# A second condition on when VectorE score tiles are held back, with a share of 0.29 and eight played orders

## The chip, the cores and the metric

The kernel runs on one core of a Trainium2 chip. The core has TensorE (PE, matrix products into PSUM banks), ScalarE (ACT), VectorE (DVE), GpSimd (POOL), and SyncE (SP), which here only issues DMAs. Each engine takes its own instructions in the order in which they were written, and waits on semaphores for the others. The metric is the device time of one execution in microseconds; it is the median of several runs.

## The reference

The inputs are 2048 rows of 640 numbers for each of two independent parts, and the output sets the two results side by side.

Part A is a state-space layer (SSM). With 640 complex states, it computes for every row t

```
h_t = Lam_bar * h_(t-1) + B_bar x_t          (one complex recurrence for each state)
y_t = 2 Re(C h_t) + Dskip * x_t
```

Part B is attention with 32 query heads of 20 numbers and a single key and value head for all of them:

```
scores = q k^T / sqrt(20)      32 heads x 2048 queries x 2048 keys
p = softmax(scores);  o = p v;  result = o wo
```

The exponential over 32 x 2048 x 2048 scores is most of the elementwise work; everything that multiplies goes through TensorE.

## The kernel before

**Tiles.** The scores are cut into 2048 tiles of 128 keys x 512 queries. There are 32 blocks (four spans of 512 queries by eight groups of four heads), and a block has 16 key chunks x 4 heads = 64 tiles. `tile_n` counts the tiles that have been handed out so far. TensorE computes up to three score tiles at once, side by side in its rows, into a PSUM tensor of three banks called SC; this is a *fill*, and there are two such tensors that take turns. A profile shows a fill as three SC matmuls.

**Two ways to the exponential.** Most tiles are done by ScalarE: one ACTIVATE (L1213) reads two or three banks of SC, takes the exponential, and writes bf16 to PR. The other tiles are done by VectorE, by an approximation in integers: a TENSOR_SCALAR (L652, by way of `fill_d`, L1390) turns a score into the bits of a bf16 number, a power of two with a straight line between. Three more copies of this tile with other integers added (`copy`, L1493) are made by POOL (INT64_ADD, L1507, two tiles at a time) or by VectorE, and a weighted sum over the four is close to the exponential. The weights are folded into four scaled copies of the values (VS). These tiles lie in BIG, in slots called DR: 20 at first and 41 later (`NDS`, `MORE`); one VectorE tile takes four of them until its products are done.

**Products.** TensorE multiplies each exponentiated tile by the values (PV): one matmul for a ScalarE tile (PR with VP), four for a VectorE tile (BIG with VS). Each such matmul uses 32 of the array's columns, and four of them, one for each head of the block, run side by side into one bank.

**The SSM part** is cut into 4 spans of 512 rows by 5 groups of 128 states. One such *unit* (`unit_task` L2009, `unit_rest` L2032) is a series of matmuls (xaT with BA and BT), and then on VectorE: the product with a table (prod<-MB,tab), an addition, two scans (L2041), the carry (ctmp, hst), a second product with the table, an edge column (L2067, or a MEMSET L2070 in the first span), and last the addition into W. Output products with C (`y_task`, L2090) follow. Units, output products, projections and softmax sums are *tasks*; most of them share one PSUM bank (MB), one after another (`manager`, L2224). Before the first unit, C is scaled on VectorE in some forty steps (`scale_c`, L1948).

**The order of the work is played out before the kernel is written.** `Schedule` (L49 on) is a planner: it has a duration for every step, and for each engine it picks, at each moment, the step with the lowest priority number whose operands are there. A fill has 0, a VectorE tile in a fill's third bank (`P1OWN`) 0.42, a task's matmuls 0.95, PV products 2.0 (0.9 when buffers run short). What the planner finds is the fixed order of each engine's instructions on the chip. `planned` (L493) plays the order from several seeds; each seed but the first moves the due times of tasks by up to 12 tiles at random. It keeps the one whose end is earliest by the planner's own durations.

**When VectorE gets a tile.** For every fill, `want_own` (L1262) decides whether the third bank goes to VectorE (then ScalarE takes two banks) or to ScalarE (then it takes three). It says no when the VectorE tiles so far would pass `SHARE` x (tile_n - 16), when two earlier ones still wait, when four slots aren't free, and when `behind` (L1273) is true. `want_d` (L1351), for a VectorE tile in the one free MB bank, has the same conditions on share, slots and `behind`. Each unit has a due time in tiles: 260 for the first, and then some 43 or 87 tiles apart up to 1693. `behind` is true when `tile_n` is more than `LAG` = 120 past the due time of the first unit whose last step (the addition into W) hasn't started. While it is true, no VectorE tile is begun. `hurry` (L2081) marks the SSM steps of a unit as `late` from 40 tiles past its due time; the steps that scale C are marked from tile 150. A late step moves ahead of most other VectorE work.

`Schedule.ready(op)` (L117) gives the time from which a step's operands are there, or None as long as some step that it needs hasn't been begun. It doesn't ask for a step's gate (a condition such as a free buffer).

Of the kernel before, what the change touches and what calls it, by code (L numbers as in the profile page):

```python
# [406 lines left out]
S, D, NC, H, DH = 2048, 640, 5, 32, 20  # L407
# [8 lines left out]
class Build:  # L416
# [4 lines left out]
    NRD = 3  # L421
    NDS = 20
    MORE = 21
    SHARE = 0.28

    SHIFTS = ((0, 0.2421875), (32, 0.201171875), (64, 0.169921875), (96, 0.142578125))

# [60 lines left out]
        self.early = [b for b in self.banks if b not in rest]  # L488

    SPREAD = 12.0  # L490
    PLANS = 4

    def planned(self):  # L493

        best = None
        for seed in range(self.PLANS):
            plan = copy.copy(self)
# [764 lines left out]
    def want_own(self):  # L1262
        if self.tile_n >= NTILE - self.LAST or self.d_count + 1 > self.SHARE * (self.tile_n - 16) or self.behind():
            return False
        if sum(1 for o in self.firsts if o.start is None) >= self.WAITING:
            return False
        self.firsts = [o for o in self.firsts if o.start is None]
        return len(self.d_free()) > len(self.SHIFTS) - 1
# [4 lines left out]
    def behind(self):  # L1273

        while self.next_unit < NQB * NC:
            w = self.w_op.get(divmod(self.next_unit, NC))
            if w is None or w.start is None:
                return self.tile_n > self.unit_due[divmod(self.next_unit, NC)] + self.LAG
            self.next_unit += 1
        return False  # L1280

# [69 lines left out]
    def want_d(self, taken=0, own=0):  # L1351
        s = self.s
        if self.tile_n >= NTILE - self.LAST or self.d_count + taken + own + 1 > self.SHARE * (self.tile_n - 16):
            return False
# [944 lines left out]
```

## Time and profile before

| | |
|---|---|
| median of three runs | 734.45 us (734.43 to 736.88) |
| the profiled execution | 734.64 us; its span 732.8 us |
| PE matmul, busy | 708.3 us (97%) |
| PE weight load, busy | 253.0 us (35%) |
| ACT, busy | 712.4 us (97%) |
| DVE, busy | 602.0 us (82%) |
| POOL, busy | 408.8 us (56%) |
| ACTIVATE PR<-SC over two banks, over three banks | 509 and 169 instructions (and one over a single bank) |
| VectorE tiles (TENSOR_SCALAR BIG<-SC and BIG<-MB) | 485 + 37 = 522 of 2048 |

The profiled execution took 0.19 us more than the median, and 1.8 us of it lie outside the span. Two engines are busy almost throughout, so that neither total tells which of them sets the pace. The ends of matmuls in a trace are modelled, and instructions of ACT and DVE overlap a little with the next (a duration includes the way in and out); starts are the safer thing to measure. A window's table gives for each engine its busy time and in brackets the number of instructions.

### The profile page before, as it was taken

How to read it: one execution, taken by the hardware profiler on the slowest of the kernel's cores; microseconds unless marked ns; L12 is line 12 of the kernel's file. 1: busy time of each engine (PE TensorE's matmuls, PEld its weight loads, DVE VectorE, ACT ScalarE, POOL GpSimd, SP SyncE). 2: the span in 40 equal slices, each digit the busy share in tenths (PEclk: the TensorE clock that was granted, in tenths of full speed). 3: DMA queues.
4: the chain of work that ended last, by engine and by line, in shares of the span. 5: the costliest groups of instructions: out<-in, count | busy, mean ns of one | idle time of the engine just before them, and what ended most of it. 6: DMA issues, size and time to landing. Idle time of an engine off the chain costs nothing.

```text
span 732.8 us, 26675 instructions
## 1 busy us (share of the span) xinstructions
PE 708.3 (97%) x11268; PEld 253.0 (35%) x11271; DVE 602.0 (82%) x1178; ACT 712.4 (97%) x703; POOL 408.8 (56%) x686
## 2 busy tenths in 40 slices
PE   8999999998999999999999999999999999999997
PEld 4322223233443432333333333233333333342233
DVE  7767999897677697778988998988889998876873
ACT  6899999999999999999999999999999999999995
POOL 3366564530046377586663746566645665687860
PEclk9799999999999999999999999999999999999999
DMA  9403543366121010100110010101100001100001
GB/s 204 68 27 107 133 110 99 76 138 97 31 60 26 13 30 24 38 23 18 40 41 23 16 26 26 42 21 34 34 20 10 19 8 40 37 24 18 19 21 38
DMA packets 78090, 34.44 MB, mean 47 GB/s; under 512 B 58852, under 2 KB 77972, under 8 KB 77972
## 3 DMA queue, kind: packets, MB, share of 16 engines
q1 hardware_dynamic: 76352, 32.34, 18.6%
q8 instruction: 90, 1.47, 0.8%
q10 hardware_dynamic: 1620, 0.39, 0.3%
q14 instruction: 28, 0.23, 0.1%
HBM read 11.53 MB, written 9.75 MB: 29 GB/s over the span
## 4 chain that ended last, share of the span: by engine, by line
ACT 52%; PE 45%; DVE 2%; DMA 1%; issue 1%; ACTq 0%
ACT PR L1213 51%; PE MB L637 16%; PE SC L637 15%; PE MB L633 12%; PE SC L633 1%; DMA BIG<-in_B_wq_dram 1%; DVE prod L647 0%; DVE BIG L652 0%; DVE mab L887 0%; DVE pvsb L647 0%; PE SC L929 0%; ACTq L618 0%; DVE g L2041 0%; DVE QT L652 0%; DVE pvsb L1574 0%
## 5 line engine op out<-in xcount | busy, mean ns | idle before, releaser
L1213 ACT ACTIVATE PR<-SC 128x1024 bf16<-128x1024 f32 (+1 forms) x679 | 697.5, 1239 | 5.1 <-PE SC L637 3.6
L1507 POOL INT64_ADD BIG<-BIG x659 | 397.9, 619 | 292.5 <-DVE BIG L652 171.8
L652 DVE TENSOR_SCALAR BIG<-SC 128x512 int16<-128x512 f32 x485 | 325.8, 686 | 70.1 <-PE SC L637 64.3
L637 PE MATMUL SC<-QT,KT 32*128 32x512 bf16 x2011 | 267.1, 386 | 14.6 <-ACT PR L1213 10.1
L637 PE MATMUL MB<-BIG,VS 128*32 128x512 bf16 x2088 | 244.0, 384 | 0.0
L637 PE MATMUL MB<-PR,VP 128*32 128x512 bf16 x1526 | 211.6, 386 | 0.5 <-DVE pvsb L1574 0.3
L637 PEld LDWEIGHTS SC<-QT,KT 32*128 32x128 bf16 x2011 | 68.0, 91 | 254.4 <-ACT PR L1213 178.1
L637 PEld LDWEIGHTS MB<-BIG,VS 128*32 128x32 bf16 x2088 | 59.1, 95 | 64.8 <-issue 47.3
L637 PEld LDWEIGHTS MB<-PR,VP 128*32 128x32 bf16 x1526 | 51.6, 95 | 54.8 <-issue 41.5
L652 DVE TENSOR_SCALAR BIG<-BIG 128x1024 int16<-128x1024 int16 (+1 forms) x136 | 48.8, 405 | 7.6 <-PE MB L637 5.7
L633 PE MATMUL MB<-CT,W 128*32 128x320 bf16 (+2 forms) x1040 | 51.4, 301 | 0.8 <-DVE prod L647 0.5
L633 PE MATMUL MB<-xaT,BT 128*32 128x256 bf16 x800 | 35.4, 275 | 0.0
L647 DVE TENSOR_TENSOR prod<-MB,tab 128x1024 bf16<-128x1024 f32 x20 | 24.3, 1217 | 13.0 <-PE MB L633 12.9
L633 PE MATMUL MB<-xaT,BA 128*32 128x256 bf16 x800 | 32.7, 274 | 0.0
L633 PE MATMUL MB<-CA,W 128*32 128x512 bf16 (+1 forms) x640 | 32.0, 302 | 0.7 <-issue 0.4
L652 DVE TENSOR_SCALAR BIG<-MB 128x512 int16<-128x512 f32 x37 | 25.2, 682 | 3.7 <-PE MB L637 2.4
L633 PE MATMUL MB<-WO,OP 128*32 128x128 bf16 (+1 forms) x576 | 27.8, 297 | 0.2 <-DVE pvsb L647 0.2
L633 PEld LDWEIGHTS MB<-CT,W 128*32 128x32 bf16 x1040 | 20.9, 96 | 18.2 <-issue 10.2
L633 PE MATMUL MB<-BIG 128*32 128x512 bf16 x340 | 26.7, 397 | 0.0
L1755 DVE CAST stg<-MB 128x512 bf16<-128x512 f32 x35 | 23.9, 683 | 1.7 <-PE MB L633 1.3
L1574 DVE CAST pvsb<-MB 128x512 bf16<-128x512 f32 x31 | 21.2, 684 | 3.8 <-PE MB L637 3.7
L2041 DVE TENSOR_TENSOR_SCAN g<-sc,hst,prod 128x256 bf16<-128x256 f32 x30 | 22.3, 754 | 0.1
(162 smaller groups left out, 388.2 us busy)
## 6 DMA issues: line engine op xcount, KB each, us to landing
out_dram<-stg SPq DMA_DIRECT2D x31, 128.0 KB, 1.8
qd<-BIG SPq DMA_DIRECT2D x20, 128.0 KB, 1.9
QT<-qd SPq DMA_DIRECT2D x28, 80.0 KB
OP<-pvsb SPq DMA_DIRECT2D x105, 20.0 KB
rdP<-recs SPq DMA_DIRECT2D x105, 20.0 KB
W<-in_A_B_re_dram SPq DMA_DIRECT2D x10, 160.0 KB, 2.6
W<-in_A_B_im_dram SPq DMA_DIRECT2D x10, 160.0 KB, 2.6
lbd<-W SPq DMA_DIRECT2D x10, 160.0 KB, 2.4
```

The source lines that it names most:

```text
L633: r = e.matmul(out[32 * j:32 * j + 32], lhsT=lhsT[:, 32 * j:32 * j + 32], rhs=rhs, start=start, stop=stop, tile_position=(0, 32 * j), skip ...
L637: return lambda e: e.matmul(out, lhsT=lhsT, rhs=rhs, start=start, stop=stop, **kw)
L647: return lambda e: e.tensor_tensor(out, a, b, op)
L652: return lambda e: e.tensor_scalar(out, a, s1, s2, op0=op0, op1=op1)
L1213: ex = self.act(lambda e: e.activation(dst, t[:, 0:512 * n], ACT.Exp, scale=1.0 / UNIT), 0.8333 * 512 * n + 64, table="exp", deps=[op], re ...
L1507: op.fns.append(lambda e: e.int64_add(words(dst), words(src), add))
L1574: ev = self.dve(lambda e: e.tensor_copy(p.pvsb[:, slot, :], bank.ap), 645, deps=[op], reads=[bank.key], writes=[f"pvsb{slot}", f"pvsb{slot ...
L1755: ev = self.dve(lambda e: e.tensor_copy(st, bank.ap), 645, deps=[prev], reads=[bank.key], writes=[key], prio=self.EV, gate=(lambda: last.e ...
L2041: o = self.dve(lambda e, ri=ri, init=init: e.tensor_tensor_scan(p.g[:, u, ri, :], rdec, p.prod[:, 1, 0, ri, :], init, ALU.mult, ALU.add), ...
```

## The change

The two limits on the planner are new (share 0.29 for 0.28, eight seeds for four), and `behind` has a second condition: besides the unit being more than 120 tiles past due, some step that waits in VectorE's list must be marked late and have all its operands begun. Where the late unit's steps aren't there yet (their matmuls haven't run, so that the first product isn't begun), VectorE tiles are no longer held back. No instruction is new. What changes is how many tiles VectorE does, when, and with it the whole planned order.

```diff
-    SHARE = 0.28
+    SHARE = 0.29
...
-    PLANS = 4
+    PLANS = 8
...
         while self.next_unit < NQB * NC:
             w = self.w_op.get(divmod(self.next_unit, NC))
             if w is None or w.start is None:
-                return self.tile_n > self.unit_due[divmod(self.next_unit, NC)] + self.LAG
+                return self.tile_n > self.unit_due[divmod(self.next_unit, NC)] + self.LAG \
+                    and any(o.late and self.s.ready(o) is not None for o in self.s.pending["dve"])
             self.next_unit += 1
         return False
```

## The prediction

> **What bounds the kernel now.** I read first the engines' totals, then the forms of ScalarE's instruction, then a table of windows, and last the order of VectorE and of PE inside them.
>
> ```profile
> L1213 ACT ACTIVATE PR<-SC 128x1024 bf16<-128x1024 f32 x509 | 480.5, 1119 | 4.9 <-PE SC L637 3.6 <-PE MB L637 0.3
> L1213 ACT ACTIVATE PR<-SC 128x1536 bf16<-128x1536 f32 x169 | 236.9, 1606 | 0.2 <-PE MB L637 0.2
> ```
>
> These are ScalarE's exponentials by shape. In the order of time one starts a median of 0.904 us after a two-bank one (mean 0.935) and 1.33 us after a three-bank one: 509 x 0.935 + 169 x 1.335 = 701.5 us, and they run from 20.4 to 721 us. ScalarE is thus never free, and a fill with a VectorE tile in it (two banks for ScalarE) is 1.335 - 0.935 = 0.40 us shorter than one without.
>
> ```profile
> core 0: us, PE busy (x) PEld busy (x) DVE busy (x) ACT busy (x) POOL busy (x), PEclk, DMA share, GB/s
> 80.00:120.00 40.00, 37.29 (x485) 11.51 (x481) 37.29 (x76) 39.96 (x39) 21.49 (x35) 1.00 0.45 118
> 120.00:153.50 33.50, 32.80 (x431) 9.62 (x428) 29.01 (x56) 32.92 (x33) 21.12 (x35) 1.00 0.41 93
> 153.50:178.00 24.50, 19.50 (x313) 7.84 (x305) 22.73 (x49) 24.50 (x20) 0.00 (x0) 1.00 0.63 122
> 178.00:204.00 26.00, 24.62 (x519) 12.37 (x516) 15.25 (x35) 26.00 (x21) 0.00 (x0) 1.00 0.23 52
> 204.00:720.00 516.00, 510.03 (x8426) 182.03 (x8422) 433.23 (x786) 514.39 (x512) 325.23 (x539) 1.00 0.10 26
> ```
>
> In these windows ACT and PE are both full; from 204 us on PE idles 6.0 us in 516. Is PE's busy time real? Its order at 686 us:
>
> ```profile
> 686.14 0.39 PE L637 MATMUL SC<-QT,KT 32*128 32x512 bf16 x3
> 686.46 0.61 PE L637 MATMUL MB<-BIG,VS 128*32 128x512 bf16 x8
> 687.01 0.39 PE L637 MATMUL SC<-QT,KT 32*128 32x512 bf16 x3
> 687.33 0.83 PE L633 MATMUL MB<-CA,W 128*32 128x512 bf16 x12
> 688.10 0.39 PE L637 MATMUL SC<-QT,KT 32*128 32x512 bf16 x3
> ```
>
> Fills are 0.87 and 1.09 us apart: 0.32 for the scores, 0.55 for eight matmuls (two rounds of four) and 0.77 for twelve. A round of four is 0.77 - 0.55 = 0.22 us, and changing between scores and the rest costs about 0.11 each way. Nothing is left between them. The hold looks like this on VectorE:
>
> ```profile
> 151.51 0.68 DVE L652 TENSOR_SCALAR BIG<-SC 128x512 int16<-128x512 f32 x1
> ...
> 177.55 0.49 DVE L647 TENSOR_TENSOR CT<-W,CT 128x640 bf16<-128x640 bf16 x1
> 178.00 0.06 DVE L2070 MEMSET W<- 128x2 bf16 x1
> 181.44 1.23 DVE L647 TENSOR_TENSOR prod<-MB,tab 128x1024 bf16<-128x1024 f32 x1 [3.37 <-PE MB L633]
> ...
> 185.81 0.42 DVE L647 TENSOR_TENSOR W<-prod 128x512 bf16<-128x512 bf16 x1
> 186.18 0.06 DVE L2070 MEMSET W<- 128x2 bf16 x1
> 186.65 0.69 DVE L1574 CAST pvsb<-MB 128x512 bf16<-128x512 f32 x1 [0.41 <-PE MB L637]
> 189.71 1.23 DVE L647 TENSOR_TENSOR prod<-MB,tab 128x1024 bf16<-128x1024 f32 x1 [2.37 <-PE MB L633]
> ...
> 203.85 0.68 DVE L652 TENSOR_SCALAR BIG<-SC 128x512 int16<-128x512 f32 x1
> ```
>
> No VectorE tile for 52 us. Counting tiles by their starts, tile 380 (due time 260 + 120) falls at 153.5 us, and every later hold too begins where the count passes a unit's due time + 120: 210, 225, 240.5, 271, 301, 330, 386, 444, 527 and 587 us.
>
> **Part 1, the condition.** A held stretch opens only where no late step has its operands begun. From 153.5 to 178 us the scaling of C is a chain in which the next step is always ready: no change there. After that a unit's column step is ready at once but takes 0.06 to 0.16 us; what opens is the wait for the unit's matmuls: 178.1-181.4, 186.2-189.7, 194.3-197.6, then 240.5-248.4 (product at 248.36) and 527-532 us. In the other holds the first product starts before or within 3 us of the hold's start, so a late step is ready throughout. At one fill per 0.94 to 1.33 us that is 3 + 3 + 3 + 7 + 3 = 19 more fills with a VectorE tile.
> - On ScalarE: 19 x 0.40 = 7.6 us less. This is the one end.
> - On PE: each such tile has four products in place of one, three quarters of a round: 0.75 x 0.22 = 0.16 us, together 3.0 us more. This is the other end, if PE alone sets the pace.
> - Each tile takes 0.40 + 0.16 = 0.56 us of PE's time, and PE idles 1.4 us in 178-204, 0.03 in 240.5-253 and nothing in 527-538. That feeds 2.5 tiles: 2.5 x 0.40 = 1.0 us. The other tiles are paid back: their products queue behind tasks, slots come free later, and later fills are refused. I take **-1.0 us**, nearest to PE's row, because it has no idle time to give.
> - On VectorE each tile is 0.69 us (19 x 0.69 = 13 us), in stretches where it idles 3.4 + 2.8 + 3.1 us and more. Queued behind such a tile are the unit's first product and the PV bank's copy to pvsb: at worst 0.69 us late in five gaps, 3.4 us of delay to the SSM chain. That lengthens holds by as much, about three tiles or 1.2 us in ScalarE's terms, nothing in PE's.
> - POOL gets 19 x 3 / 2 x 0.62 = 18 us of copies, hidden (it stood still for these 52 us). SP gets no new DMA and none is moved in its queue by this condition itself; the issues of sums and OP wait for pvsb alone, by the same 0.69 us at most.
>
> A rule is to be weighed here. The Trainium skill (Perfetto Trace Analysis, Identifying the Most-Contended Engine) says that TensorE's headroom is not to be judged by its matmul busy share but by that of the weight loads. That is 253.0 of 732.8 us, 35%, which leaves room, and by the rule part 1 would be worth its whole 7.6 us. The rows at 686 us differ: starts follow each other with nothing between, so I go by them.
>
> The same skill (SBUF — State Buffer, Who interferes with whom) speaks against the change: VectorE with two SBUF inputs and a GpSimd op that reads SBUF exclude each other for a whole instruction. The trace has one: OP<-OP,rdP took 0.66 us at 241.06, while POOL's INT64_ADD of 0.61 began at 240.83, against a mean of 0.43. By the rule alone a unit's second step would be blocked up to 0.62 us in each of the five gaps, 3.1 us in the SSM chain; by the row 0.23 x 5 = 1.2 us.
>
> **Part 2, the share.** At 40, 80, 120 and 160 us the count of VectorE tiles is 6, 37, 70 and 96 at tiles 42, 160, 283 and 393, below 0.28 x (tile - 16) by 1, 3, 5 and 10; from 200 us on by 35 to 53. Up to three tiles are handed out and not begun, so the limit binds until about 130 us and never after. 0.29 allows 0.01 x (393 - 16) = 3.8 tiles more: bounds 0 and -1.5 us (3.8 x 0.40), or +0.6 us by PE's 0.16. PE idles 2.7 + 0.7 us in 80-153.5, enough for six. But only 20 slots are there then. I take two tiles, **-0.8 us**.
>
> **Part 3, the orders.** No row shows another order. What an order can change is how far ScalarE's starts are stretched over 0.904 and 1.33: 0.4 to 1.6 us in a stretch of 40 us, a spread of about 0.4, so 0.4 x sqrt(18) = 1.7 us for a whole order. Bounds: -1.7 and +1.7 us (the planner chooses by its own durations, and the new condition reshuffles every seed). The best of eight instead of four: I take **-0.5 us**, a third of it.
>
> **Sum**: -1.0 - 0.8 - 0.5 = -2.3 us. The profiled execution goes from 734.64 to 732.3; it stood 0.19 above the median, so the median goes from 734.45 to **732.1 us**, with a range of its own of 729.5 to 735 (order +-1.7, share 0 to -1.5).
>
> **The rivals.**
> - *ScalarE is the bound after all.* For it: ACT's 514.39 of 516 us, and PE takes its tasks only in the holes left by fills. Each tile also brings the due times 0.40 us nearer, and the holds at 210, 225, 271, 301 us, which don't open, grow; I take off 6 tiles: 13 x 0.40 + 1.5 + 0.5 = 7.2 us, **727.2 us**.
> - *PE's debt (slower).* For it: PE's 510.03 of 516 us, and the last SSM output product still runs at 708 us, so work put off has nowhere to go. If slots don't refuse the later tiles and VectorE goes toward its new limit, 0.29 x 2012 = 583 tiles, there are up to 61 more: 61 x 0.16 = 9.8 us. I take half, 30 tiles: +4.8, **739.3 us**. It decides once tiles begun beyond the 2.5 that idle time feeds exceed about 15 (15 x 0.16 = 2.4 us, which eats the sum above). Against it: slots have kept the count 50 under the old limit.
> - *The condition does next to nothing.* `ready` ignores gates, and an edge column or a waiting step of the next unit may keep it true in the planner's time. Then parts 2 and 3 remain: 733.1; without an effect of the share, **734 us**.
>
> **How the numbers follow.** Likeliest 0.38; ScalarE bound 0.25; PE's debt 0.22; nothing 0.15. About 0.5% (3.7 us) is what a measurement here can tell from no change: faster means under 730.8, slower over 738.1. Faster: 0.23 of the 0.25 and 0.10 of the 0.38, 0.33. Slower: 0.18 of the 0.22 and 0.03 from an order that falls badly, 0.21. The rest, 0.46, is the same. The range takes in most of ScalarE's case and half of PE's: 726.5 to 739.5 leaves out about 0.08 below and 0.11 above.
>
> **What the next profile would show.** Step 1 right: VectorE tiles between 178 and 204 us, about nine, and between the column step and the first product of later units; still none from 153 to 178. The payback: the total stays near 522 to 530, PE's idle time in 178-204 is gone, ACT two-bank starts are stretched more than 0.935. ScalarE's case: over 535 tiles, and still 0.935. PE's debt: the last SSM output product later than 709 us against the end of the exponentials, or a longer tail than 12 us. The share: a count of VectorE tiles two to four higher at tile 283. The prediction is wrong if PE has room that its starts hide, or if the new order shifts something outside these terms, in the first 40 us or in the tail.

## The result, and the profile after

The changed kernel takes 732.06 us (median of 18 runs, 730.51 to 734.83). The kernel before, run again on the same chips beside it, takes 735.52 us (18 runs, 733.18 to 739.5). The ratio is 0.9953, with a 95% interval of 0.9936 to 0.9969: 3.5 us less, within the 0.5% that the prediction called no difference, though the interval leaves 1 out. At equal granted clock of TensorE it is 4.2 us less (how this is reckoned stands at the head of the experiments). The profiled execution took 732.94 us, its span 731.2 us.

Which steps moved? First the forms of ScalarE's exponential in the kernel after (count | busy us, mean ns | idle before, releasers):

```profile
L1213 ACT ACTIVATE PR<-SC 128x1024 bf16<-128x1024 f32 x517 | 489.7, 1120 | 5.2 <-PE SC L637 4.6 <-PE MB L637 0.2
L1213 ACT ACTIVATE PR<-SC 128x1536 bf16<-128x1536 f32 x162 | 228.4, 1584 | 0.0
```

Eight more fills are of two banks and seven fewer of three (509 and 169 before). The starts are as far apart as they were: a mean of 0.9354 us after a two-bank one and 1.3324 after a three-bank one. 516 x 0.9354 + 162 x 1.3324 = 698.5 us (the last of the 517 has no next start), against 701.3 before (509 x 0.9346 + 169 x 1.3350; the prediction's 701.5 comes from rounded means). ScalarE's own list is thus 2.8 us shorter. The two profiled spans differ by 1.6 us only (732.8 and 731.2), since in the profile after the list begins 1.5 us later, at 21.9 us for 20.4: from 10 to 20 us its granted clock is 0.85, where it was 1.00 before. VectorE does 492 + 36 = 528 tiles, six more than before.

The table of windows, after, with the same windows as in the prediction:

```profile
core 0: us, PE busy (x) PEld busy (x) DVE busy (x) ACT busy (x) POOL busy (x), PEclk, DMA share, GB/s
80.00:120.00 40.00, 34.66 (x455) 10.73 (x447) 39.19 (x81) 40.00 (x40) 20.30 (x34) 1.00 0.47 108
120.00:153.50 33.50, 32.18 (x410) 10.21 (x411) 32.48 (x63) 33.28 (x33) 18.95 (x32) 1.00 0.40 101
153.50:178.00 24.50, 22.03 (x306) 7.42 (x299) 22.89 (x56) 24.50 (x20) 0.00 (x0) 1.00 0.67 128
178.00:204.00 26.00, 25.17 (x507) 12.28 (x505) 21.26 (x42) 26.00 (x23) 5.97 (x10) 1.00 0.28 64
204.00:720.00 516.00, 512.66 (x8485) 182.03 (x8486) 429.96 (x765) 515.07 (x512) 335.76 (x556) 1.00 0.10 26
```

From 204 us on PE idles 3.3 us in 516, where it idled 6.0 before; ACT is as full as it was. In 178 to 204 us there are 23 ACTIVATEs where there were 21, and POOL, which stood still there, makes ten copies: VectorE tiles begin in the old hold. They show in VectorE's order, after:

```profile
181.66 0.49 DVE L647 TENSOR_TENSOR CT<-W,CT 128x640 bf16<-128x640 bf16 x1
182.88 0.69 DVE L652 TENSOR_SCALAR BIG<-SC 128x512 int16<-128x512 f32 x1 [0.73 <-PE SC L637]
184.22 0.69 DVE L652 TENSOR_SCALAR BIG<-SC 128x512 int16<-128x512 f32 x1 [0.65 <-PE SC L637]
185.31 0.69 DVE L652 TENSOR_SCALAR BIG<-SC 128x512 int16<-128x512 f32 x1 [0.39 <-PE SC L637]
185.91 1.22 DVE L647 TENSOR_TENSOR prod<-MB,tab 128x1024 bf16<-128x1024 f32 x1
187.05 0.68 DVE L652 TENSOR_SCALAR BIG<-SC 128x512 int16<-128x512 f32 x1
...
192.00 0.42 DVE L647 TENSOR_TENSOR W<-prod 128x512 bf16<-128x512 bf16 x1
```

The hold opens as soon as C is scaled (CT<-W,CT ends at 182.15) and the first unit's product isn't there yet. Three tiles go in front of this product and a fourth behind it. The same chain ran from 177.55 (CT<-W,CT) by 181.44 (product) to 185.81 (W<-prod) before: now the first unit is done at 192.0, 6.2 us later. Of these, 2.5 us have nothing to do with the tiles: the kernel with the share alone (e2) has C scaled 2.5 us earlier than this one, and this one is behind it by the same 2.5 us at tile 50 already.

### The profile page after: what moved, and what is told of

It reads as the page before. It is cut to its first block, busy times and chain, and to the rows that moved or that the text cites. A ratio compares the mean times of both kernels' runs of the same rounds, so it can differ in the third digit from the quotient of the medians.

```text
span 731.2 us, 26574 instructions
## 1 busy us (share of the span) xinstructions
PE 709.3 (97%) x11222; PEld 252.0 (34%) x11225; DVE 606.2 (83%) x1175; ACT 709.7 (97%) x703; POOL 418.3 (57%) x701
## 4 chain that ended last, share of the span: by engine, by line
ACT 55%; PE 41%; DVE 1%; DMA 1%; issue 0%; ACTq 0%; POOL 0%
ACT PR L1213 55%; PE MB L637 14%; PE SC L637 14%; PE MB L633 12%; DMA BIG<-in_B_wq_dram 1%; PE SC L633 1%; DVE BIG L652 0%; PE SC L929 0%; DVE mab L887 0%; POOL BIG L1508 0%; ACTq L618 0%; DVE QT L652 0%; DVE brow L652 0%; DVE pvsb L1575 0%; DVE BA L1720 0%
## 5 line engine op out<-in xcount | busy, mean ns | idle before, releaser
L1508 POOL INT64_ADD BIG<-BIG x674 | 407.5, 620 | 280.4 <-DVE BIG L652 143.9
L652 DVE TENSOR_SCALAR BIG<-SC 128x512 int16<-128x512 f32 x492 | 330.6, 686 | 83.6 <-PE SC L637 78.5
L637 PE MATMUL MB<-BIG,VS 128*32 128x512 bf16 x2112 | 255.9, 384 | 0.2
L637 PE MATMUL MB<-PR,VP 128*32 128x512 bf16 x1520 | 217.9, 388 | 0.2 <-ACT PR L1213 0.2
L637 PEld LDWEIGHTS MB<-BIG,VS 128*32 128x32 bf16 x2112 | 62.9, 95 | 68.6 <-issue 46.4
L652 DVE TENSOR_SCALAR BIG<-BIG 128x1024 int16<-128x1024 int16 (+1 forms) x127 | 46.3, 408 | 4.1 <-PE MB L637 3.4
L633 PE MATMUL MB<-xaT,BA 128*32 128x256 bf16 x800 | 35.3, 274 | 0.0
L633 PE MATMUL MB<-WO,OP 128*32 128x512 bf16 (+1 forms) x512 | 25.6, 306 | 0.0
L633 PEld LDWEIGHTS MB<-xaT,BA 128*32 128x32 bf16 x800 | 19.6, 96 | 9.6 <-issue 6.3
```

What stands on the lines that cost most here:

```text
L633: r = e.matmul(out[32 * j:32 * j + 32], lhsT=lhsT[:, 32 * j:32 * j + 32], rhs=rhs, start=start, stop=stop, tile_position=(0, 32 * j), skip ...
L637: return lambda e: e.matmul(out, lhsT=lhsT, rhs=rhs, start=start, stop=stop, **kw)
L652: return lambda e: e.tensor_scalar(out, a, s1, s2, op0=op0, op1=op1)
L1508: op.fns.append(lambda e: e.int64_add(words(dst), words(src), add))
```

## The experiments

All the comparisons are with the kernel before, run in the same set: medians of 735.62 us (26 runs) for the first four kernels, 736.25 (10) for the next four and 735.82 (18) for the last four. The planner's own end is given too. It isn't a measured time but the moment at which the last step ends by the planner's durations, 723.12 us for the kernel before.

The theory at the start was the prediction's: PE is the bound, a VectorE tile is paid only out of PE's idle time, and the condition is worth little because the rest is paid back. The rivals were that ScalarE is the bound and more VectorE tiles are worth their 0.40 us; and that the gain is not of the condition at all, but of another order or of the share.

**The granted clock.** One thing differs between executions of the same kernel and has to be taken off before small differences are read. In every profile TensorE's granted clock (PEclk) stands at 0.50 for a stretch that begins between 25 and 29 us, and its length varies. The window from 24 to 44 us of the kernel before, of e1, of e2 and of the kernel after, in turn:

```profile
core 0: us, PE busy (x), PEclk, DMA share, GB/s
24.00:44.00 20.00, 19.62 (x207) 0.74 0.18 47
24.00:44.00 20.00, 19.62 (x223) 0.83 0.19 49
24.00:44.00 20.00, 19.62 (x211) 0.74 0.18 41
24.00:44.00 20.00, 19.38 (x188) 0.66 0.15 30
```

That is about 10.4, 6.8, 10.4 and 13.6 us at half clock ((1 - 0.74) x 2 x 20 = 10.4). The time follows: of the 54 executions of the kernel before that have their clock on record, the one with the lowest mean clock (0.985) took 739.85 us, the eleven with the highest (0.995) a median of 733.97. One straight line fitted to all 157 executions, with a level for each kernel, gives 0.51 us for each 0.001 of mean clock and leaves a scatter of 0.55 us. On it the three chips agree within 0.4 us for the kernel before. The executions of two kernels don't have the same clock on average (0.9888 in e2, 0.9926 in the kernel before beside it). So the differences are also given at equal clock, by this line, uncertain by 0.3 to 0.5 us at 95% (0.8 in e5 and e6, which have two executions, and 0.7 in e8; the profiles of e5 and e8 have a second stretch at half clock near 180 us, whose price isn't shown). Why the stretch is longer in one execution than in another, and whether a kernel's own order has a part in it, isn't shown.

### The condition alone (e1_condition, e9_condition_order2)

```diff
 # the kernel after
-    SHARE = 0.29
+    SHARE = 0.28
-    PLANS = 8
+    PLANS = 4
```

> The second condition alone: share 0.28 and four seeds, as before. Theory PE (TensorE sets the pace, tiles let through are paid back later): some seven more VectorE tiles in 178-204 us and ten in 240-253, most of them missing again within 40 us, total 524 to 530; 1 to 2.5 us faster than before. Rival ScalarE (each tile kept is worth 0.40 us and nothing has to be paid back): over 535 tiles and 5 us or more. Rival that the gain came from the choice among orders and the share: no faster than before, +-1 us.

Measured: 732.8 us, ratio 0.996 (0.9946 to 0.9974), 2.9 us less (2.5 at equal clock). The planner kept its order 3, with 528 tiles. The kernel before has order 2, so the same comparison was made at this order:

```diff
 # the kernel after
-    SHARE = 0.29
+    SHARE = 0.28
-        for seed in range(self.PLANS):
+        for seed in (2,):
```

> The condition alone, share 0.28, with the order of seed 2, the seed that the kernel before keeps, so that the tasks' due times are jittered alike. Theory: the condition is worth 1 to 3 us in any order; the planner's own end is 1.0 us earlier than that of the kernel before: 0.5 to 2 us faster. Rival: what the condition alone gained came from another order: +-0.5 us.

Measured: 734.07 us, ratio 0.9972 (0.9955 to 0.9988), 2.1 us less (1.5 at equal clock), with 523 tiles.

The condition by itself is worth 2 to 3 us; at equal clock 1.5 to 2.5 of the 4.2. Where does it come from? VectorE's instructions that read SC, in the windows around the openings; e1 first:

```profile
core 0: us, DVE busy (x), PEclk, DMA share, GB/s
178.00:204.00 26.00, 5.57 (x9) 1.00 0.19 44
204.00:240.50 36.50, 14.52 (x22) 1.00 0.15 37
240.50:253.00 12.50, 6.02 (x9) 1.00 0.04 10
253.00:280.00 27.00, 10.69 (x16) 1.00 0.09 19
527.00:538.00 11.00, 3.84 (x6) 1.00 0.07 15
```

and the kernel after:

```profile
178.00:204.00 26.00, 5.51 (x8) 1.00 0.28 64
204.00:240.50 36.50, 12.33 (x18) 1.00 0.15 37
240.50:253.00 12.50, 7.57 (x12) 1.00 0.05 11
253.00:280.00 27.00, 10.06 (x15) 1.00 0.09 19
527.00:538.00 11.00, 4.98 (x9) 1.00 0.04 10
```

The kernel before has 1, 27, 1, 22 and 1 in these windows. The three openings that the prediction named are there, with 8 + 8 + 5 = 21 more tiles in e1 and 7 + 11 + 8 = 26 after. The window behind each of the first two has fewer: 22 and 16 for 27 and 22 in e1, 18 and 15 after. At the end six tiles are left.

The time at which a given tile starts tells the same. All numbers are differences to the kernel before in us (the fill that holds the tile), and in brackets the difference in VectorE tiles begun by then:

| tile | e1, condition | after |
|---|---|---|
| 50 | -1.2 (0) | +2.7 (+1) |
| 300 | -1.2 (0) | -0.3 (+7) |
| 500 | -4.0 (+7) | -2.0 (+8) |
| 700 | -5.2 (+9) | -1.8 (+8) |
| 1000 | -2.0 (+3) | +1.7 (+1) |
| 1400 | -0.1 (-1) | +2.0 (0) |
| 1500 | -3.5 (+5) | -1.0 (+6) |
| 2040 | -3.9 (+6) | -1.4 (+6) |

(At tile 50, where no VectorE tile is held yet, e1's profiled execution was 1.2 us ahead and the one after 2.7 behind, in step with the half-clock stretches above. From there to tile 2040 e1 gains 2.7 us and the kernel after 4.1.) The openings at 178 to 248 us bring 4 us by tile 700 in e1, and by tile 1400 they are given back whole. The opening at 527 us takes 3.0 to 3.4 us off the stretch from tile 1400 to 1500 (35.4 us before, 32.0 in e1, 32.4 after), and nothing takes this back: from tile 1500 to 2040 it is 175.9 us in both, 176.3 before. So in these two kernels the net gain is that of the last opening. It isn't so in every order. In e9 the three windows hold 9, 12 and 7 tiles and the stretch from tile 1400 to 1500 is 3.5 us shorter too, but 3.1 of them are gone again at tile 2040; in e3 (the kernel after in another order, below) the stretch is 0.9 us shorter and 0.8 are gone. What decides whether this gain stays isn't shown. In e1 and after, the units behind it are not late: the additions into W at 536.5 and 559.7 us before are at 536.6 and 557.7 in e1, at 532.2 and 550.6 after, and so no hold that follows gets longer.

What pays back? Not the slots. In the planner, the answers to the question whether VectorE may have the third bank were:

```
                yes   no: held   no: two waiting or no slots
before          475         89                            69
after           480         92                            60
condition (e1)  487         96                            52
```

(Five and four are refused for the share, before and after.) The openings take some 20 refusals off the hold's 89, and yet it ends with more; the slots refuse fewer. The units are later, so the following holds are longer: the first eight additions into W are at 185.8, 193.9, 202.0, 215.3, 230.2, 252.2, 275.0 and 304.6 us before; at 188.3, 195.5, 205.3, 218.9, 228.1, 254.6, 278.4 and 310.5 in e1; at 192.0, 198.8, 207.3, 222.7, 234.1, 257.0, 279.1 and 312.6 after. Why they are later shows in VectorE's order in e1:

```profile
176.32 0.49 DVE L647 TENSOR_TENSOR CT<-W,CT 128x640 bf16<-128x640 bf16 x1
177.37 0.69 DVE L652 TENSOR_SCALAR BIG<-SC 128x512 int16<-128x512 f32 x1
178.90 0.69 DVE L652 TENSOR_SCALAR BIG<-SC 128x512 int16<-128x512 f32 x1 [0.84 <-PE SC L637]
179.77 0.69 DVE L652 TENSOR_SCALAR BIG<-SC 128x512 int16<-128x512 f32 x1 [0.18 <-PE SC L637]
180.76 0.69 DVE L652 TENSOR_SCALAR BIG<-SC 128x512 int16<-128x512 f32 x1 [0.29 <-PE SC L637]
181.37 1.21 DVE L647 TENSOR_TENSOR prod<-MB,tab 128x1024 bf16<-128x1024 f32 x1
182.50 0.68 DVE L652 TENSOR_SCALAR BIG<-SC 128x512 int16<-128x512 f32 x1
183.09 0.41 DVE L647 TENSOR_TENSOR prod<-prod 128x512 bf16<-128x512 bf16 x1
...
188.27 0.42 DVE L647 TENSOR_TENSOR W<-prod 128x512 bf16<-128x512 bf16 x1
```

The scaling of C ends 1.2 us earlier than before (as the whole profile is 1.2 us ahead) and the first product starts at the same time (181.37 and 181.44), and yet its unit ends 2.5 us later: from the product to W it takes 6.9 us for 4.4, with a score tile, a copy to pvsb and waits between its steps.

### The share alone (e2_share)

```diff
 # the kernel before
-    SHARE = 0.28
+    SHARE = 0.29
```

> The share alone: 0.29 in the kernel before, four seeds. Theory: the limit binds only until about 130 us; two tiles more at tile 283 than before (72 against 70), the same total within 4, 0.8 us faster at most; from 200 us on nothing. Rival: with more VectorE tiles in the stretch in which C is scaled, the SSM chain starts later: 0 to 2 us slower. Either way the order that is kept may be another one (+-1.7 us).

Measured: 737.76 us, ratio 1.0027 (1.0012 to 1.0042), 2.0 us more, but +0.2 at equal clock, which is no difference. At a mean clock of 0.986 and 0.988 e2 took medians of 738.79 and 737.76 us, and the kernel before, on another chip, 738.68 and 737.78; the profiled executions, both at 0.993, have spans of 732.6 and 732.8 us. The planner kept order 0, with 520 tiles.

The share does what the prediction says of it, more so: seven tiles more are begun by tile 300 (the prediction took two, its upper end was 3.8), and tile 350 starts at 141.5 us for 142.8. The lead is 1.4 us at tile 500. But by tile 1400 it is 2.1 us behind, with no more VectorE tiles than before, and by tile 2040 1.4 us; the rest is made up in the tail. In its VectorE order the same first stretch is:

```profile
179.15 0.49 DVE L647 TENSOR_TENSOR CT<-W,CT 128x640 bf16<-128x640 bf16 x1
182.80 1.23 DVE L647 TENSOR_TENSOR prod<-MB,tab 128x1024 bf16<-128x1024 f32 x1 [3.16 <-PE MB L633]
187.79 0.42 DVE L647 TENSOR_TENSOR W<-prod 128x512 bf16<-128x512 bf16 x1
```

C is scaled 1.6 us later than in the kernel before, and the first unit ends 2.0 us later: tiles begun early delay the scaling. So the early lead is real and is given back; a loss over the whole isn't shown. The share at one fixed order wasn't measured.

### The orders (e3_after_order0, e4_before_order6, e11_after_four)

```diff
 # e3: the kernel after; e4: the kernel before
-        for seed in range(self.PLANS):
+        for seed in (0,):      # e3
+        for seed in (6,):      # e4
 # e11: the kernel after
-    PLANS = 8
+    PLANS = 4
```

> The changed kernel, but with the order of the unjittered seed alone in place of the best of eight. Theory: orders spread by some 1.7 us on the chip and the planner's ranking carries over in part: 1 to 3.5 us slower than the changed kernel, so within 2 us of the kernel before. Rival: the ranking says nothing on the chip: as fast as the changed kernel, +-1 us.

> The kernel before, with the last of eight orders by the planner's ranking in place of the first. Theory as for the run before: 1.7 to 3.5 us slower than the kernel before. Rival: +-1 us.

> The changed kernel with four seeds in place of eight; it then keeps the order of seed 1, whose end by the planner is 0.2 us later than that of the changed kernel. Theory (the planner's ranking carries over to within some 1.5 us): within 1.5 us of the changed kernel, 2 to 5 us faster than before. Rival (eight orders bring the gain that the share and condition don't): no faster than 1.5 us over before.

Measured: e3 734.44 us, ratio 0.9989 (0.9977 to 1.0); e4 740.24 us, ratio 1.0056 (1.0035 to 1.0076); e11 731.14 us, ratio 0.9932 (0.9911 to 0.9954). At equal clock they are at -1.4, +2.5 and -4.7 us.

An order can cost 4.1 us (e4, a bad one in the kernel before; 2.5 at equal clock) and 2.6 us (e3 against after; 2.8 at equal clock), more than the prediction's 1.7. But eight orders rather than four bring nothing that can be measured: with four the kernel after has order 1 instead of 7, and the intervals overlap. Without the condition and at a share of 0.28, eight orders give the kernel before itself: order 2 has the earliest planned end among the eight as it has among four.

### No hold at all (e5_never_held)

```diff
 # the kernel before
-                return self.tile_n > self.unit_due[divmod(self.next_unit, NC)] + self.LAG
+                return False
```

> The kernel before with no hold at all: the function that tells whether the SSM is behind always says no. Theory PE: VectorE takes tiles up to its share of 0.28 (some 560 in place of 522), PE gets 40 x 0.16 = 6 us more work, and the SSM chain runs late on VectorE and PE, so that its last output products stand at the end: 5 to 20 us slower. Rival ScalarE: 40 tiles x 0.40 = 16 us faster.

Measured: 757.45 us, ratio 1.0301 (1.0241 to 1.0362), 22 us more (20.6 at equal clock), with 562 VectorE tiles.

Here PE's debt is seen whole. At tile 1400 this kernel had begun 45 more VectorE tiles and was 12.6 us ahead of the kernel before (493.5 against 506.1 us). Then ScalarE stops. Its waits:

```profile
ACT PR L1213 <- PE MB L637: 34.3, 7, 32.3
```

(us in total, times, the longest). Its order in time:

```profile
488.80 18.94 ACT L1213 ACTIVATE PR<-SC 128x1024 bf16<-128x1024 f32 x19 [0.61 <-PE MB L637]
540.05 35.51 ACT L1213 ACTIVATE PR<-SC 128x1536 bf16<-128x1536 f32 x35 [32.31 <-PE MB L637]
```

And what PE does in these 32 us:

```profile
510.80 0.73 PE L633 MATMUL MB<-xaT,BA 128*32 128x256 bf16 x20 [0.80 <-DVE stg L1755]
...
514.50 1.26 PE L633 MATMUL MB<-WO,OP 128*32 128x512 bf16 x20 [1.33 <-DVE prod L647]
516.60 0.73 PE L633 MATMUL MB<-xaT,BA 128*32 128x256 bf16 x20 [0.84 <-DVE stg L1755]
...
520.30 2.34 PE L633 MATMUL MB<-CT,W 128*32 128x512 bf16 x40 [1.33 <-DVE prod L647]
```

It works off overdue units, output products and attention outputs through the one task bank, and waits 0.8 to 1.3 us for a copy or a product of VectorE's between them. The debt of too many VectorE tiles is not 0.16 us of products for each; it is the SSM chain, which the hold exists to keep on time. 12.6 us gained and 32 us of stop leave +20, near the measured +22.

### What sets the pace (e6_pe_more, e7_pe_less, e8_act_less)

All three keep the order of the kernel before. The first adds work to PE, 69 rounds of four products with zero weights between tiles 500 and 2000, 69 x 0.216 = 14.9 us by the distance of their starts in its trace:

```diff
+        self.n_pv += 1
+        if self.n_pv % 6 == 0 and 500 < self.tile_n < 2000 and ...:
+            op.fns += [self.mm(bank.tensor[32 * j:32 * j + 32, bank.off:bank.off + 512], p.VZ[:], p.KT[:, 0:512],
+                               False, False, ...) for j in range(4)]
```

> The kernel before, every engine's order unchanged, with 69 rounds of four extra products by zero weights (512 columns each) put behind PV products between 203 and 688 us: 69 x 0.21 = 14.7 us more for PE, nothing for the others. Theory PE: PE has 6 us of idle time in these 516, so 9 to 14 us slower. Rival ScalarE: PE's starts hide room between fills; 0 to 4 us slower.

Measured: 743.75 us, ratio 1.0115 (1.0079 to 1.0151), 8.5 us more (9.2 at equal clock).

The second takes some 21 us of PE's work away, in the output products, of which it leaves half of the columns in four of five groups uncomputed:

```diff
+            mid = (lo + hi) // 2 if k < 4 else hi
+            some = bank.cols(o0, o0 + mid - lo)
...
-                    prev = self.pe([self.mm(to, W[:, c, ri, at:at + 128], m[:, ri, c, lo:hi], n == 0, False)],
+                    prev = self.pe([self.mm(some, W[:, c, ri, at:at + 128], m[:, ri, c, lo:mid], n == 0, False)],
```

> The kernel before, order unchanged, with half of the columns left out of the SSM's output products with C and of the skip product that goes with them, in four of the five column groups (that half of those outputs isn't computed): some 200 rounds of four at 0.107 us less for PE, 21 us between 250 and 710 us. ScalarE's starts can shrink from a mean of 0.935 and 1.335 to 0.904 and 1.33 at best, 16 us in all. Theory PE: 5 to 12 us faster, in the stretches in which output products run. Rival ScalarE: 0 to 2 us.

Measured: 735.53 us, ratio 0.9983 (0.9961 to 1.0005), 1.3 us less (0.5 at equal clock), not to be told from no change.

The third takes from ScalarE: from the 31st ACTIVATE on, it does 448 of the 512 columns of each bank and leaves the rest as it was. A bank is 1.33 - 0.904 = 0.426 us of the distance between starts, so that an eighth of it, over 1465 banks, is about 78 us:

```diff
+        if self.n_ex > 30:
+            dst = p.PR[:, h.index:h.index + n, 0:448]
+            src = src.rearrange("p (n c) -> p n c", n=n)[:, :, 0:448]
```

> The kernel before, order unchanged, with the exponential from the 31st instruction on over 448 of each 512 columns (the rest of a tile is what lay there before, so the attention output is wrong in an eighth of the queries): 64 / 1.2 = 53 ns less for each bank, some 0.0533 x 1480 = 79 us less for ScalarE. Theory PE (PE sets the pace from 204 us): 5 to 20 us faster, most of it where fills have three banks. Rival ScalarE: 60 us or more faster. Anything between says that both are at their limit and which stretch belongs to which.

Measured: 729.02 us, ratio 0.9888 (0.9826 to 0.995), 8.2 us less (9.0 at equal clock).

The window from 204 to 720 us, with the columns of the tables above, has e6, e7 and e8 in turn:

```profile
204.00:720.00 516.00, 512.60 (x8558) 183.90 (x8550) 429.14 (x777) 510.11 (x504) 321.92 (x532) 1.00 0.11 26
```

```profile
204.00:720.00 516.00, 495.71 (x8426) 182.43 (x8422) 433.59 (x786) 514.25 (x512) 325.28 (x539) 1.00 0.11 26
```

```profile
204.00:720.00 516.00, 512.11 (x8579) 182.89 (x8575) 433.98 (x792) 484.21 (x514) 325.85 (x539) 1.00 0.11 26
```

The prediction held that PE alone sets the pace. That falls with e7: 21 us less for PE (14.3 by the busy time of the window) give 1.3, and ACT stays at 514.25 of 516 us. That ScalarE alone sets it falls with e8: 78 us less give 8.2, ACT drops to 484 and PE stays at 512. Its waits in e8 are on PE:

```profile
L1218 ACT ACTIVATE PR<-SC 128x896 bf16<-128x896 f32 x479 | 420.5, 918 | 28.2 <-PE SC L637 21.6 <-PE MB L637 3.7
L1218 ACT ACTIVATE PR<-SC 128x1344 bf16<-128x1344 f32 x169 | 209.0, 1301 | 12.2 <-PE SC L637 10.2 <-PE MB L637 0.8
```

Neither alone sets the pace; both are at their limit together, which fits an order that ties them fill by fill. Relieving one gives a tenth, or less than a tenth, of what was taken off (1.3 of 21, 8.2 of 78), and loading PE costs more than half (8.5 of 14.9). Lightening both at once wasn't tried. The rule of the Trainium skill that the prediction weighed (Perfetto Trace Analysis, Identifying the Most-Contended Engine) would read PE's 35% of weight loads as headroom (the section names the share of peak arithmetic beside it, which wasn't worked out here); e6 shows that little of it is there. The gaps at 686 us were the better guide.

### Another way to hold less (e10_longer_lag, e12_after_lag)

If how much is held matters and not where the hold opens, one number in the old rule should do the same:

```diff
 # e10: the kernel before; e12: the kernel after
-    LAG = 120
+    LAG = 135
 # e12 alone
-    PLANS = 8
+    PLANS = 24
```

> The kernel before with one number changed: the SSM counts as behind from 135 tiles past due in place of 120; no second condition, share 0.28, four seeds. Theory: what the condition brings is only that tiles are held in fewer fills while the SSM chain still ends in time, so that a somewhat longer wait does the same: the planner's own end is 2.6 us earlier; some 530 tiles, 1.5 to 4 us faster. Rival (it matters where the hold opens, namely when no late step is ready): no faster, +-1 us, since the steps that are ready are delayed too.

> A version meant to beat both: the changed kernel with 135 tiles in place of 120 and 24 seeds. By the planner its end is 0.8 us earlier than the changed kernel's and 4.3 earlier than that of before. Theory: 3 to 5.5 us faster than before, level with the changed kernel or up to 2 us faster. Rival (both engines are full, so nothing more comes from moving holds): within 1 us of the changed kernel.

Measured: e10 731.2 us, ratio 0.9936 (0.9913 to 0.9959), with 531 VectorE tiles; e12 732.25 us, ratio 0.994 (0.9918 to 0.9962), with 528.

At equal clock they are 3.9 and 5.3 us below the kernel before, the kernel after 4.2. A lag of 135 tiles gives the old rule as much as the whole change gives, and the two together give about 1 us more than either at equal clock, though not by the ratios; e12 also had 24 orders to choose from, and which of the two brings it isn't shown. In e10 the eighth addition into W is at 308.9 us for 304.6, but the last copy of an SSM output is at 708.5 us as before (708.9), and the count of tiles is nine higher. That fits a hold that was a little too long; whether a lag between 135 and no hold at all is better yet wasn't tried.

### The planner's own end against the chip

| kernel | planner's end, difference to before | measured, from the ratio | measured, at equal clock |
|---|---|---|---|
| after | -3.5 | -3.5 | -4.2 |
| e1 condition | -1.5 | -2.9 | -2.5 |
| e2 share | +0.1 | +2.0 | +0.2 |
| e3 after, order 0 | -0.2 | -0.8 | -1.4 |
| e4 before, order 6 | +3.4 | +4.1 | +2.5 |
| e5 never held | +21.7 | +22.1 | +20.6 |
| e9 condition, order 2 | -1.0 | -2.1 | -1.5 |
| e10 lag 135 | -2.6 | -4.7 | -3.9 |
| e11 after, four orders | -3.35 | -5.0 | -4.7 |
| e12 after, lag 135 | -4.3 | -4.4 | -5.3 |

The column from the ratio is (ratio - 1) x 735.6 us. In these ten the planner is right within 2.1 us by the ratio and within 1.3 us at equal clock, over a span of 27.

## Why the prediction came out where it did

The predicted time was 732.1 us and 732.06 was measured. That they agree so closely is luck: the kernel before came out at 735.52 us this time, 1.1 above the 734.45 from which the prediction started, so that the change is -3.5 us (-4.2 at equal clock) where -2.3 was forecast. The terms of the sum fared as follows.

- **Part 1, the condition (-1.0): right in sign and in where the holds open, too small.** Alone it measured -2.9 us (the best of four orders) and -2.1 (the same order), at equal clock -2.5 and -1.5. The openings stand where they were predicted: the window 178 to 204 us holds 8 tiles for the forecast nine, none are in 153.5 to 178, and the total of 528 is within 522 to 530. The step that failed is the one that limits the gain to PE's idle time inside the openings (2.5 tiles). Over the whole span, PE's idle time with its zero-weight filler products fell from 32.0 to 28.1 us in e1 and 26.5 after: the new order found room elsewhere too, so six tiles stayed instead of 2.5. In e9 this time is 32.5 us and one tile stayed; where its gain comes from stays open.
- **The payback was right, its cause wrong.** "Slots come free later, and later fills are refused" did not happen: fewer questions are refused for slots. The SSM chain is later and the next holds are longer. The prediction had this effect as a side line ("at worst 0.69 us late in five gaps, 3.4 us of delay"); in e1 the first unit alone loses 2.5 us between its product and W.
- **ScalarE's starts are not stretched.** The prediction expected more than 0.935 after a two-bank one as the sign of PE's limit; it stays 0.935. The sign stood for ScalarE's case, and so does the account 698.5 against 701.3 us.
- **Part 2, the share (-0.8): nothing where measured alone, +0.2 at equal clock.** The local gain was there and larger than taken. What was missing is what these early tiles delay: the forty steps that scale C, which stand behind them on VectorE (1.6 us later in e2; 4.1 in the kernel after, 2.5 of which are its later start).
- **Part 3, the orders (-0.5): nothing.** Four orders serve as well as eight. The bound of 1.7 us on an order's effect was too narrow: 4.1 us in e4, 2.5 at equal clock.
- **What bounds the kernel.** "PE alone" was wrong, and so was its rival "ScalarE after all" as a sole bound: both at once (e6, e7, e8). PE's idle time in 178 to 204 us is gone in e1 (0.24 us), not after (0.83, for 1.38 before).
- **PE's debt** showed in its sign without its price: the last copy of an SSM output is at 712.6 us for 708.9, and the time from tile 2040 to the end of the span is 14.8 us for 15.0. In e5 it shows with its price, from the SSM chain and not from the products' 0.16 us each.
- **The block between VectorE and GpSimd** (the Trainium skill, SBUF — State Buffer, Who interferes with whom) was priced at 1.2 us by the row. In the kernel after, the second step of a unit (prod<-prod) takes a mean of 451 ns for 424 and the addition into W 440 for 416: 20 x (27 + 24) ns = 1.0 us in all. The seven second steps that have a GpSimd copy beside them take a mean of 512 ns, the thirteen others 418. The trace agrees with the rule in direction; a block for a whole instruction isn't the usual case.

The three parts were taken as -1.0, -0.8 and -0.5. At equal clock they measure -1.5 to -2.5, +0.2 and nothing, and the whole is -4.2: they don't add. With the condition in place and four orders, the larger share is 2.1 us better (e11 against e1), in another order each; how much of this is the share and how much the order isn't shown.

## What to carry to other kernels

When two engines are both full and an order fixed beforehand ties them, ask not which one is the bound but what a piece of work costs both; here a tenth or less came back of what was taken from one of them. When two kernels differ by half a per cent, look at the granted clock of each execution first: here 0.01 of it was worth 5 us, more than the change. When a rule that holds work back is loosened, follow the chain that it protects: here the openings gained 4 us by tile 700 and had lost them by tile 1400, with that chain later and the next holds longer. Before giving such a rule a second condition, try its one number.

## What was unexpected

- 21 us of matmul work taken from an engine that is busy 97% of the span gave 1.3 us (0.9983, 0.9961 to 1.0005), while 14.9 us more on it cost 8.5.
- The planner's durations carry over to the chip within 2.1 us out of 735 for ten different orders, and within 1.3 at equal clock. For the share alone the planner had +0.1 us, and +0.2 was measured at equal clock, where the count of tiles gave -0.8.
- Most of the scatter between executions of one kernel goes with TensorE's granted clock, and in the profiles most of that is lost in one stretch of 7 to 17 us near 30 us, at half clock.
